# A new written-out order for all five engines, with two groups of constants of its planner changed

## The chip, the cores and the metric

The kernel runs as one program on one core of a Trainium2 chip. The metric is device time in microseconds (us). Before the change three runs took 282.60, 282.91 and 282.98 us, a median of 282.91. The interval that a repeat of this kernel stays in is about 0.2%, some 0.57 us.

## The reference

Eight batches of eight heads of decayed (retention) attention without softmax, 576 positions of 64 features each, feed a two-layer block with a gate `h * cos(h)`. The outputs of the attention are laid side by side by head, which gives 4608 tokens of 512 features.

```python
scores = scale * np.matmul(q, k.transpose(0, 1, 3, 2))
...
ret = scores * Dmat[None, :, :, :]
x = np.matmul(ret, v) ...        # 8 x 8 x 576 x 64, then 4608 x 512
h = x @ w_in                     # 512 x 2048
g = h * np.cos(h)
return (g @ w_out).astype(np.float32)   # 2048 x 512
```

## The kernel before

**Attention in units.** A unit is 256 positions of one batch with all its heads, named (batch, part); the last 64 positions of four batches make a unit of their own. For a unit q, k and v are loaded as float32 by SP (L585), turned into bf16 tiles `qnat`, `natk` and `natv` by POOL, DVE or ACT (L575, L624; v and q are multiplied by powers of the decay), and transposed, by TensorE in the first four units (L648) and by a DMA transpose in the others (L663). TensorE then makes scores (L694, `bk<-qt,kt`), DVE masks them (L743, `pt`), TensorE adds up the running states (L694, `bk<-natv,natk`, copied by ACT to `sba`, `sbb`, `sbr`) and the outputs (L694, `bk<-pt,natv` and `bk<-qt,sba`), and ACT and DVE copy these to `xt`. The matmuls of L694 are small, 64x64 weights with 64 or 128 columns, four of them side by side in the array, so that many instructions pass in a short time.

**Nine token blocks of 512.** Block j takes two units. The first layer is L908 (`bk<-xt,win`, with ACT's cosine in L917 and DVE's product in L920) in blocks 0 to 2, and a scheme of seven products instead of eight (L1037, with L1020, L1022 and L1026 for the gate) in blocks 3 to 8. The second layer uses seven products throughout: L1177 multiplies `gt`, sums `s` made by DVE (L1108, L1114) and weight sums `tw` (L1086); DVE and ACT put the result together in `os` (L1166, L574), and SP stores it (L1065). `win` and `wout` are each loaded in four slabs by POOL (L888, L892), as 512 KB of bf16 each, on the software DMA queue. Six loads of q, k and v go out at once; the loads of unit (0,1) wait until slab 2 of `win` has landed, since `unit((0, 1), gate=[("win", self.NEXT)])` has NEXT = 2, and the loads of unit (2,0) wait for slab 2 of `wout`.

**What sets the order.** `graph` makes some 1500 tasks, each for one engine. `lay` gives each task its rank from the table ORDER, two characters a task, and so fixes the order on each engine: an engine takes its tasks by rank, none overtakes another, and the semaphores follow from the data. `run` then goes through this order with planned times. These decide which buffer a task gets, how many idle matmuls (L517, `bk<-one`) are put in where TensorE is thought to wait, and which POOL operations are held back behind a DVE operation that ran shortly before (`push`). The table itself was found beforehand with the same planned times, and is written in as a constant.

**Instruction fetches in the planner.** TensorE's program is read in blocks of 256 instructions, where a matmul counts two (its weight load and itself) and a task some 0.2 to 0.4 for its waits. In `run` the fetch of block k is requested when instruction 128+256k is reached, and instruction 450+256k can't run before `usable[k]`. `FETCH` holds the times: 3200 ns after the request or 1500 ns after the planned end of the transfers, whichever is later, plus a last part.

**Slabs in the planner.** `load_w` gives each slab a time on the software queue (`dma`) and a time from its last packet to the semaphore (`tail`).

Of the kernel before, what the change touches and what calls it, by code (L numbers as in the profile page):

```python
# [371 lines left out]
class Kernel:  # L372
# [12 lines left out]
    ORDER = (
        "#####$#$#$#%#%#$#######%#&#&#%#$#&#'#)#(#'#)#,#+#'#.#7#/#*#/#'#+#*#,#(#-#.#&#&#%#*#)#(#-#(#)#*#0#2#0#1#3"
        "#2#1#,#7#V#8#/#7#'#(#,#)#-#.#G#@#K#H#*#0#/#L#C#J#G#+#2#1#+#N#O#K#L#M#N#P#E#S#P#T#H#Q#,#3#5#f#[#^#R#-#8#6"
        "#b#W#V#L#.#<#;#5#+#4#U#I#S#3#-#5#E#>#E#6#.#6#@#8#>#4#5#<#=#4#?#<#3#;#>#6#=#H#A#J#;#2#:#:#1#9#B#9#@#9#0#8"
        "#C#=#C#R#G#R#F#?#F#Q#F#P#I#B#I#D#<#D#A#:#A#?#;#B#M#D#O#4#7#9#:#/#>#=#0#?#@#1#A#G#6#m#o#j#k#m#l#l#_#r#u#s"
        "#a#`#_#d#y#p#^#i$'#w#]#Q#[#v#b#s$'#l$%$/#s$/#Z#N#W$3#v$1#e#Z#c$+#r$-#j#^#h$$#i#{#x#d#u$.#q$0#_#S#]$1#t$."  # L390
        "#[#O#X$(#m$&#W#J#T#{#h#|#\\#T#\\$*#n$)#Y#M#Y$&#k$(#|#g#x$,#p$+#X#K#U#y#f#z#a#U#`#z#j$##c#X#f#w#c#t#i#]#g$)"
        "#o$*#Z#b#V#a#q#e#o#n#`#d#Y#q#t#r#k#p#e#g#h#\\$#$%$$#n#u#v#8$-$0#w#O#2#D#B#5#I#C#3#E#H#<$5$7$7$9$8$3$6#z$?"
        "$$$#$@$%#|#4#9#F#K#7#J#N#=#;#M#L#C#:#>#O#R#A#Q#T#?#@#S#P#F$>$B$?$<$A$@$F$,$+$G$'$&$\\$?$Z$O$0$I$[$>$V$_$C"
        "$[$S$6$Q$U$7$P$K$*$D$Z$=$U$J$($G$M$-$J$L$1$L$R$5$N$Q$3$K$Y$<$T$X$:$R$T$@$Y$2$4$,$6$5$;$>$=$4$8#x$2$:$:$;"
        "$<#y$9$=#{$A$D$B$C$E$C#`$H$I$)#P$N$H$F$.$/$P$2$4$V$;$9$W$8$S#B#G#W#Z#E#X#V#D#M#Y#`#Q#J#N#^#a#H#c#[#I#L#\\"
        "#d#V$]$X$W$B$A$b$D$G$c$E$^$o$l$k$M$R${$Y$Z$|$W$s#S#K#f#l#R#e#j#U#X#g#o#[#T#\\#i#t#Y#w#x#W#Z#k#q#g%'$w$x$^"
        "$a%.$l$m%/$f$|#U$E#]$M#_$d#b$n$`$b$e$f$`$F$k$J$f$K$i$n$N$r$p$b#p$p$m$Q#h$y$V$t$s$O$t$P$x$U$r$v$S$z$u$[#n"
        "$w$q$X#m%($_$y%%$\\%&$]%*$e%#%)$`%-${$j#s%+$z$d#r%1$k%(%,$c%3$i%2$h%%%0$g%4%&$n#v%6%'$p#u%9$q%.$]$_$\\$a$c"
        "$o$O$g$d$e$H$^$a$h$h$i$I$g$j$L$l$m$j%#%$$v#o$q$u$T#f%)%+%1%/%=$r%>$s%@$v%5%A$t%D%8%%$(%B%4%,$*%L%$%?%E$y"
        "%G$|%M%#%>%H${%K%<%($&%N%=%.$)%P%&%A%S%*%U%-%Y%1%G%V%2%]%H%7$,%Z%F%<$.%d%=%P%[%3%_%6%`%9%L%^%5%c%K%>$1%e"  # L400
        "%N%E$2%g%?%Q%$%*%0%2%:%6%9%7%5%7$o%:%?%3%<%F$z%;%C$w%O%T%B%I%J%;$&%X%\\%4#q%8%-%,$u$x%Q%)%'%R%+%@#d#]#{#y"
        "#a$$#z#^#e$##|#i#b#k$%$0#h$3$-#_#c$'$+#v%W%D%C%/%0%a%8%:%b%;%J%M%S%V%T%k%B%m%D%o%G%[%n%C%q%Y%H$8%r%Z%K$<"
        "%u%M%b%z%N%{%O&'%S%e&$%P&(%d%W$?&%%c%Z$A&-%Y%i&&%R&)%U&*%T%f&,%V&3%j%`$C&.%h%c$D&6%e%q&/%X&1%]&2%\\%k&4%^"
        "&9%p%h$F&7%n%d$E&>%i%v%E%I%U%X%^%]%W%\\%f%i%A%p%x%`%l%t%L%j%s%I&#&+%g%y%|%a$?&0&5%_$=%h%O%R%@%F%v%Q%[%w%J"
        "%_#l#m$7$/#n$:$5#p#j$4$6#|#s#t$9$=#w$@$B#r#u$;$>$+&8%o%m%b%a&<%f%l&=%g%r%s%u%{%x&@%j&E%o&C%n%|&D%m&I&%%x"
        "$H&H&$%v$G&O%u&,&M%s&P%w&V&#&/&Q%y&W&1&($N&U&.&&$K&a&+&;&X&$&Y&%&[&'&6&]&*&c&5&1$P&\\&4&2$R&h&5&A&b&,&g&0"
        "&i&3&=&f&/&j&?&8$S&k&<&9$U&t&:&D%l%t%w&#&)%y&+&'&;&?%k&A&B%z&G&L%q&:&F%p&R&Z&0&K&N&*$7&^&`&-$:&J&&&(%r%t"
        "&S%z%{&T%|&-$-$6#z$4$I$L$%$,$8$0$J$O$##y#x#{$W$[$9&_&2&3&)&d&e&.&7&8&9&>&:&l&4&n&7&q&<&F&o&6&r&C&K$\\&s&B"
        "&@$Y&y&?&G&u&;&v&=&z&D&Q&x&A'&&K&L$_&{&H&C$X'*&I&R'#&B')&E'(&G&V''&F'/&W&O$`',&P&M$^'6&P&\\'4&N'5&Q'8&T&f"
        "'7&R';&]&X$a':&^&[$b'>&Z&h&@&E&I&L&M&J&S&N&m&p&>&|'$&O'%'-&J&w'+&H'0'2&Y'.'3&X$@'9'=&V$>$1$$$2$'$Q$V$)$5"  # L410
        "$*$($M$T$3$.$<$/$]$Z$;'1&[&T&Z&U'<&S&_&U&`&b&c&e&d'?&W'A&Y'B&\\&i'E&^'K&n&j$e'D&k&g$d'O&c&q'F&]'H&_'P&d&t"
        "'I&`'N&p&e$c'L&r&k$f'U&i&x'M&b'T&h'Q&o'#'W&l'[&w&p$g'Y''&y$i'^&r&{'Z&n'a&t'`&s'$']&q'b&|&u$h'f'+&z$j'e&v"
        "'&&a&l&j&m&g&v&s&o'@'G&a'S'V&u'R'X&m'C'J&f'\\'c'%'_'d'($A'i'j'#$C&y&z')','*'/'-'0'g'h&w&x'o'p'.$E$B'k'n&{"
        "&|'l'm'$'q'r'1'2$F$D's't'3'%'&'v'u'5'4$H$G"
    )
# [470 lines left out]
    def load_w(self, which, s, gate, prio):  # L886
        if which == "win":
            fn = lambda e: e.dma_start(  # L888
                ap(self.WIN, 4 * DFF, 0, 128, s * 512, [DFF, 4], [1, 512]),
                bass.AP(self.w_in, s * 512, [[DFF, 128], [128 * DFF, 4], [1, 512]]))  # L890
        else:
            fn = lambda e: e.dma_start(  # L892
                ap(self.WOUT, NF * DM, 0, 128, s * 4 * DM, [DM, 4], [1, DM]),
                bass.AP(self.w_out, s * 4 * 128 * DM, [[DM, 128], [128 * DM, 4], [1, DM]]))
# [456 lines left out]
```

## Time and profile before

| what | us |
|---|---|
| three runs, median | 282.91 (282.60 to 282.98) |
| the profiled execution, own time | 284.13 |
| its span, first to last instruction | 282.4 |
| what lies around the span | 1.73 |
| TensorE (PE) matmuls busy | 270.7 |
| PE waits for `win` by DMA | 0.9 |
| PE waits that the profile calls "issue", L694 and L908 | 2.4 and 0.7 |

The profile lists busy time by engine, groups of instructions by line, and the chain of work that ended last, followed back from the end: a share of a line in the chain is time in which nothing else could have ended the program earlier. "issue" is time in which an engine waited for nothing that the profile shows. A busy PE is not a PE at its peak, since matmuls are pipelined and their ends are modelled; the distance from one start to the next says more. In views of DMA, q1 is the queue of SP's transfers, q0 the software queue on which POOL's go, and q8 carries instructions. The granted clock of TensorE was 1.00 throughout.

### The profile page before, as it was taken

How to read it: one execution, taken by the hardware profiler on the slowest of the kernel's cores; microseconds unless marked ns; L12 is line 12 of the kernel's file. 1: busy time of each engine (PE TensorE's matmuls, PEld its weight loads, DVE VectorE, ACT ScalarE, POOL GpSimd, SP SyncE). 2: the span in 40 equal slices, each digit the busy share in tenths (PEclk: the TensorE clock that was granted, in tenths of full speed). 3: DMA queues.
4: the chain of work that ended last, by engine and by line, in shares of the span. 5: the costliest groups of instructions: out<-in, count | busy, mean ns of one | idle time of the engine just before them, and what ended most of it. 6: DMA issues, size and time to landing. Idle time of an engine off the chain costs nothing.

```text
span 282.4 us, 9745 instructions
## 1 busy us (share of the span) xinstructions
PE 270.7 (96%) x4136; PEld 219.9 (78%) x4136; DVE 227.3 (80%) x394; ACT 177.5 (63%) x367; POOL 161.2 (57%) x180
## 2 busy tenths in 40 slices
PE   6779989999999999979999999999999999999995
PEld 2457568888885468868888888888888888888884
DVE  3666889988974998868997996688759899997764
ACT  4346767255247765669469875885778865778530
POOL 4640872167377683897568757981375667216330
DMA  7999999999999999999999997979816090410016
GB/s 199 249 192 262 273 171 163 300 243 263 179 187 245 204 264 206 181 221 176 251 192 208 279 238 134 168 194 175 194 32 123 6 163 2 159 69 0 2 74 224
DMA packets 122731, 49.91 MB, mean 177 GB/s; under 512 B 84800, under 2 KB 118592, under 8 KB 122688
## 3 DMA queue, kind: packets, MB, share of 16 engines
q1 hardware_dynamic: 118176, 44.84, 74.8%
q0 software_dynamic: 4224, 4.19, 9.6%
q8 instruction: 32, 0.52, 0.8%
q10 hardware_dynamic: 288, 0.26, 0.3%
q14 instruction: 11, 0.09, 0.1%
HBM read 36.70 MB, written 9.44 MB: 163 GB/s over the span
## 4 chain that ended last, share of the span: by engine, by line
PE 84%; DMA 8%; POOL 3%; issue 2%; SPq 1%; DVE 1%; ACT 1%; DVEq 0%; ACTq 0%
PE bk L1177 38%; PE bk L1037 26%; PE bk L908 11%; PE bk L694 8%; DMA stgq<-in_q_dram 3%; DMA win<-in_moe_w_in_dram 3%; DMA stgk<-in_k_dram 3%; POOL natv L624 1%; SPq L585 1%; POOL qnat L624 1%; POOL gt L1026 1%; POOL win L888 0%; ACT xt L574 0%; DVE sq L1020 0%; PE bk L648 0%
## 5 line engine op out<-in xcount | busy, mean ns | idle before, releaser
L1026 POOL TENSOR_TENSOR gt<-sq,cb 128x512 bf16<-128x512 f32 x48 | 55.8, 1172 | 49.1 <-ACT cb L1022 27.0
L908 PE MATMUL bk<-xt,win 128*128 128x256 bf16 (+1 forms) x288 | 46.3, 308 | 1.8 <-DMA win<-in_moe_w_in_dram 0.9
L624 POOL TENSOR_TENSOR natv<-stgv,wv 128x512 bf16<-128x512 f32 x36 | 37.5, 1046 | 12.5 <-DVE s L1108 4.8
L920 DVE TENSOR_TENSOR gt<-bk,cb 128x256 bf16<-128x256 f32 (+1 forms) x72 | 34.5, 507 | 12.0 <-ACT cb L917 9.3
L917 ACT ACTIVATE cb<-bk 128x256 bf16<-128x256 f32 (+1 forms) x72 | 31.2, 455 | 19.6 <-PE bk L908 16.5
L624 POOL TENSOR_TENSOR qnat<-stgq,wq 128x512 bf16<-128x512 f32 x32 | 33.5, 1052 | 16.7 <-DVE s L1114 5.6
L1037 PE MATMUL bk<-xt,win 128*128 128x256 bf16 x288 | 41.0, 273 | 0.0
L1020 DVE TENSOR_TENSOR sq<-bk,sq 128x512 f32<-128x512 f32 x48 | 32.5, 684 | 8.9 <-PE bk L1037 5.0
L908 PEld LDWEIGHTS bk<-xt,win 128*128 128x128 bf16 x288 | 26.8, 98 | 15.3 <-DVE pt L743 1.2
L743 DVE TENSOR_TENSOR pt<-bk,tr 128x512 bf16<-128x512 f32 x48 | 31.1, 682 | 8.4 <-PE bk L694 8.1
L575 POOL CAST natk<-stgk 128x512 bf16<-128x512 f32 x34 | 20.7, 614 | 28.2 <-DMA stgk<-in_k_dram 15.7
L1177 PE MATMUL bk<-wout,gt 128*128 128x256 bf16 x288 | 36.7, 273 | 0.0
L1026 DVE TENSOR_TENSOR gt<-bk,cb 128x512 bf16<-128x512 f32 x48 | 32.3, 682 | 4.0 <-ACT cb L1022 3.8
L1177 PE MATMUL bk<-wout,s 128*128 128x256 bf16 x288 | 35.6, 273 | 0.0
L1177 PE MATMUL bk<-tw,s 128*128 128x256 bf16 x288 | 35.4, 273 | 0.0
L574 ACT ACTIVATE sq<-bk 128x512 f32<-128x512 f32 x48 | 27.7, 595 | 10.0 <-PE bk L1037 8.8
L1022 ACT ACTIVATE cb<-sq 128x512 bf16<-128x512 f32 x48 | 30.0, 632 | 5.4 <-DVE sq L1020 2.9
L1022 ACT ACTIVATE cb<-bk 128x512 bf16<-128x512 f32 x48 | 28.4, 598 | 6.7 <-PE bk L1037 3.7
L1177 PEld LDWEIGHTS bk<-tw,s 128*128 128x128 bf16 x288 | 28.0, 98 | 3.6 <-DVE pt L743 0.3
L1037 PEld LDWEIGHTS bk<-xt,win 128*128 128x128 bf16 x288 | 27.9, 98 | 3.6
L1177 PEld LDWEIGHTS bk<-wout,gt 128*128 128x128 bf16 x288 | 27.6, 98 | 3.7 <-issue 0.2
L1177 PEld LDWEIGHTS bk<-wout,s 128*128 128x128 bf16 x288 | 27.7, 98 | 3.5
(80 smaller groups left out, 436.5 us busy)
## 6 DMA issues: line engine op xcount, KB each, us to landing
stgq<-in_q_dram SPq DMA_DIRECT2D x16, 512.0 KB, 6.1
out_dram<-os SPq DMA_DIRECT2D x16, 512.0 KB, 4.4
stgk<-in_k_dram SPq DMA_DIRECT2D x20, 256.0 KB, 5.6
stgv<-in_v_dram SPq DMA_DIRECT2D x20, 256.0 KB, 5.4
stgk<-in_k_dram SPq DMA_DIRECT2D x6, 512.0 KB, 6.9
stgv<-in_v_dram SPq DMA_DIRECT2D x6, 512.0 KB, 7.4
win<-in_moe_w_in_dram POOLq DMA_DIRECT2D x4, 512.0 KB, 8.0
wout<-in_moe_w_out_dram POOLq DMA_DIRECT2D x4, 512.0 KB, 7.5
```

What stands on the lines that cost most here:

```text
L574: return self.one(eng, dur, lambda e: e.activation(dst(), src(), AF.Copy), r=r, w=w, **kw)
L624: self.one(eng, 610 if eng == "dve" else 1030, lambda e, out=out, inp=inp, tab=tab, col=col, hs=hs: e.tensor_tensor(out(), inp(), ap(tab, ...
L694: return lambda e: e.matmul(out(), lhs(), rhs(), start=start, stop=True, skip_group_check=True)
L743: self.one("dve", 610, lambda e, r=r, b=b, pt=pt: e.tensor_tensor(ap(self.at(pt), 1024, 0, 128, 512 * r, [64 * ny * ny, 8 // ny // ny], [1 ...
L908: inst = e.matmul(ap(self.at(bk), 512, 0, 128, 0, [1, n]), ap(self.WIN, 4 * DFF, 0, 128, c * DFF + 128 * f, [1, 128]), ap(self.at(xt), 204 ...
L917: self.one("act", n - 15, lambda e: e.activation(ap(self.at(cb), TB, 0, 128, 0, [1, n]), ap(self.at(bk), 512, 0, 128, 0, [1, n]), AF.Sin, ...
L920: self.one("dve", 75 + n / 0.96, lambda e: e.tensor_tensor(ap(self.at(gt), NF * TB, 0, 128, f * TB + 256 * h0, [1, n]), ap(self.at(bk), 51 ...
L1020: self.one("dve", 610, lambda e: e.tensor_tensor(half(src), self.at(bank).ap(), half(src), ALU.add), r=[(bank,)], w=four(src))
L1022: self.one("act", 530 if name else 490, lambda e: e.activation(self.at(cb).ap(), ap(self.at(src), size, 0, 128, 0, [1, 512]), AF.Sin, bias ...
L1026: self.one(eng, 1120 if name else 610, lambda e: e.tensor_tensor(ap(self.at(gt), NF * TB, 0, 128, (8 * n + 2 * g) * TB + 256 * h, [TB, 2], ...
L1037: inst = e.matmul(ap(self.at(bank), 512, 0, 128, 256 * f, [1, 256]), l(c, f), rr(c), stop=True, skip_group_check=True, start=(first and f ...
L1177: inst = e.matmul(place(bank, tt), l(f, tt), rr(f), stop=True, skip_group_check=True, start=(first and f == 0 and tt < len(bank)))
```

## The change

Three things change. The constants of the planned fetch get longer by 1500 ns, for requests before 45 us (4550 to 6050 ns) and after (2550 to 4050 ns). The planned slab times change from 2750 ns (`win`) and 3000 ns (`wout`) to 3350 ns for slab 0 of either and 2750 ns for the others, and slab 3 gets a tail of 2300 ns instead of 900. And ORDER is replaced as a whole. No task is added or taken away; beside the order, only the idle matmuls (24 before, 32 now) and the buffers that a task gets can differ. The table is cut to two lines here.

```diff
-    BACKLOG, FIRST = 4000, 6000
+    BACKLOG = 4000
     SHARES = (0.65, 0.30)
-    FETCH = (3200, 1500, 2550, 2000)
+    FETCH = (3200, 1500, 4050, 6050)
...
-                    usable[k] = max(a + self.FETCH[0], dma_free + self.FETCH[1]) + self.FETCH[2] + self.FETCH[3] * (a < 45000)
+                    usable[k] = max(a + self.FETCH[0], dma_free + self.FETCH[1]) + self.FETCH[2 + (a < 45000)]
...
     ORDER = (
-        "#####$#$#$#%#%#$#######%#&#&#%#$#&#'#)#(#'#)#,#+#'#.#7#/#*#/#'#+#*#,#(#-#.#&#&#%#*#)#(#-#(#)#*#0#2#0#1#3"
+        "#####$#$#$###%#$#####&#%#%#&#%#$#&#'#(#'#(#)#*#+#'#-#)#.#*#.#'#-#+#/#+#,#/#&#&#%#)#(#*#,#(#*#(#1#2#1#3#0"
...
-                 sem=f"{which}{s}", dma=2750 if which == "win" else 3000, tail=900, prio=prio)
+                 sem=f"{which}{s}", dma=3350 if s == 0 else 2750, tail=2300 if s == 3 else 900, prio=prio)
```

**TensorE between the outputs of unit (4,0) and the scores of unit (5,0)**, about 120 to 124 us of the profiled execution. `pt`, `natv`, `qt` and `sba` belong to the small matmuls of L694, `wout,s` to the second layer, and `xt` and `xs` to the first. In the kernel before stand the last small matmuls of the outputs, four rows of large matmuls, and the first of the scores:

```order
L694 MATMUL bk2<-qt2,sba2 64x64 x2
L1177 MATMUL bk7<-wout,s5 128x256 x8
L1177 MATMUL bk7<-wout,s6 128x256 x8
L1037 MATMUL bk2<-xt1,win 128x256 x4
L1037 MATMUL bk3<-xs0,tx1 128x256 x4
L694 MATMUL bk1<-qt0,kt1 64x64 x2
```

In the changed kernel the same place begins with:

```order
L694 MATMUL bk2<-qt2,sba2 64x64 x2
L1037 MATMUL bk1<-xt1,tx4 128x256 x4
L1037 MATMUL bk6<-xt1,win 128x256 x4
L1037 MATMUL bk0<-xs0,tx1 128x256 x4
L1177 MATMUL bk7<-wout,s3 128x256 x8
L1037 MATMUL bk6<-xs1,tx2 128x256 x4
L1037 MATMUL bk0<-xs2,win 128x256 x4
L1037 MATMUL bk1<-xt1,win 128x256 x4
L1037 MATMUL bk5<-xt1,win 128x256 x4
L1037 MATMUL bk6<-xt1,win 128x256 x4
```

Four more matmuls of L1037 follow before the scores, so that 44 large matmuls stand between the two runs of small ones where 24 stood.

**POOL at the start**, where it turns the first k and v into bf16 tiles and issues the four slabs of `win`. Before:

```order
L575 CAST natk1<-stgk1 128x512
L624 TENSOR_TENSOR natv0<-stgv0,wv 128x512
L888 DMA win<-in_moe_w_in_dram 128x4x512 x2
L624 TENSOR_TENSOR natv1<-stgv1,wv 128x512 x2
L888 DMA win<-in_moe_w_in_dram 128x4x512 x2
```

In the changed kernel:

```order
L575 CAST natk1<-stgk1 128x512
L624 TENSOR_TENSOR natv0<-stgv0,wv 128x512
L888 DMA win<-in_moe_w_in_dram 128x4x512
L624 TENSOR_TENSOR natv1<-stgv1,wv 128x512
L888 DMA win<-in_moe_w_in_dram 128x4x512
L624 TENSOR_TENSOR natv1<-stgv1,wv 128x512
L888 DMA win<-in_moe_w_in_dram 128x4x512 x2
```

The second slab now goes out behind one conversion of unit (1,0), the last two behind both. By the ranks in the two tables the slabs go out as 0, 2, 3, 1 before and as 0, 3, 2, 1 now.

More of the change, by code (lines that the diff above doesn't have):

```diff
@@ L391 @@
[L391 to L410, printed above, removed]
@@ new lines @@
+        "$e%5$k$l%6$m%)#R$F#]$H#`$d#a$p$^$b$j$f$]$B$f$G$b$F$h$k$L$q$n$P#g$o$l$U#i$x$W$t$s$Q$u$R$w$T$q$v$S$z$r$X#j"
+        "$y$s$^#n%$$[$v%%$\\%&$]%+$b%$%($`%,$z$d#r%)$y$j#s%1$i%(%*$a%2$h%/$g%%%-$c%0%&$q#u%4%'$p#t%9$r%.$_$a$]$`$c"
+        "$i$P$e$d$e$H$c$h$g$i$j$I$g$l$M$m$n$k${%'$x#h$r$t$V#d%*%,%2%0%8$o%?$v%;$s%4%>$u%B%7%##|%C%6%-$,%I%(%?%E$y"
+        "%F$z%H${%:%J$|%M%<%)$%%K%;%%$(%P%+%A%S%,%T%.%X%2%F%W%0%\\%H%:$.%Y%E%9$/%a%;%P%[%3%b%8%`%7%K%_%6%d%M%A$0%g"
+        "%O%E$2%i%@%S$w${%1%3%9%+%8%=%3%7$n%=%A%5%<%G%$%@%D$w%Q%U%B%L%R%@$/%Z%e%<#p%:%/%-$t$x%N%*%&%O%'%>#c#`#{$)"
@@ new lines @@
+        "#b$*#z#^#a#v$&#m#f#e$#$'#j$+$3#_#i$$$1#v%V%C%D%/%1%]%4%=%^%5%I%J%L%R%Q%h%?%n%F%m%G%Y%k%B%o%W%O$7%q%X%H$5"
+        "%s%L%_%x%N%|%R&%%S%e%{%Q&$%b%Z$?&&%c%X$@&+%W%g&'%T&)%U&*%V%f&,%Y&0%j%\\$C&.%i%`$D&5%d%q&/%[&7%a&2%]%m&4%_"
+        "&8%o%i$F&:%p%e$E&;%h%t%G%N%V%Z%`%\\%d%]%c%f%>%v%w%^%j%z%P%p%r%J&(&-%h%y&#%a$*&1&6%c$@%l%T%U%C%D%t%K%M%u%I"
+        "%[#q#l$6$8#n$9$4#r#k$:$-$+#t#o$;$>#w$<$=#u#s$B$A$.&3%k%l%^%b&<%g%m&=%f%s%u%x&%&#&?%k&D%r&C%l%y&F%n&J&'%y"
+        "$I&L&*%|$K&N%u&+&M%t&U%z&Q%w&-&P%v&V&/&&$N&X&1&*$P&h&2&?&Y&%&Z&$&`&,&5&^&(&c&7&4$R&_&4&-$Q&l&8&A&a&+&b&."
@@ L415 @@
+        "'K&a'P&s&g$e'L&o&c$c'T&j&v'N&f'S&h'X&r'%'U&i'Y&w&s$g'W&z&z$j']&q&{'Z&m'[&o'_&t'$'^&p'a&|&v$h'b')&w$i'd&u"
+        "''&X&i&j&m&a&q&x&p'?'A&`'Q'R&u'V'\\&n'E'J&k'`'f'&'c'i'*$A'l'o'$$D&y'+'(','#'/'-'0'h'j&x&y'e'p'.$B$C'm'n&|"
+        "&{'g'k'#'q'r'2'1$E$F's'u'4'%'&'v't'5'3$H$G"
     )
```

23 lines of the change are left out of this document (15 added, 8 removed).

## The prediction

> **What bounds the kernel now.** I read the page's busy times and chain first, to see which engine ends the work.
>
> ```profile
> PE 270.7 (96%) x4136; PEld 219.9 (78%) x4136; DVE 227.3 (80%) x394; ACT 177.5 (63%) x367; POOL 161.2 (57%) x180
> q8 instruction: 32, 0.52, 0.8%
> PE 84%; DMA 8%; POOL 3%; issue 2%; SPq 1%; DVE 1%; ACT 1%; DVEq 0%; ACTq 0%
> ```
>
> TensorE is the chain, but for the start. No matmul of the computation is added or taken away, so all that an order can change is time in which TensorE stands still. Its waits, longest first, show what that is:
>
> ```profile
> PE bk L694 <- issue: 2.4, 3, 1.5
> ...
> PE bk L908 <- DMA win<-in_moe_w_in_dram: 0.9, 1, 0.9
> PE bk L908 <- issue: 0.7, 1, 0.7
> ```
>
> The largest, 2.4 + 0.7 = 3.1 us, is a wait for nothing that the trace names. The timeline of TensorE gives the places:
>
> ```profile
> 20.40 0.50 PE L908 MATMUL bk<-xt,win 128*128 128x256 bf16 x3 [0.68 <-issue]
> ...
> 38.22 0.22 PE L694 MATMUL bk<-natv,natk 64*64 64x64 bf16 x3 [0.71 <-issue]
> ...
> 125.45 0.25 PE L694 MATMUL bk<-natv,natk 64*64 64x64 bf16 x7 [1.46 <-issue]
> ```
>
> The second and third fall in the midst of one group of small matmuls, where no data is awaited. The DMA view, asked in stretches of 0.1 us, shows what ends them. These are its q8 lines from 18.0, 35.7, 44.3, 114.0 and 122.6 us on:
>
> ```profile
> q8 instruction: 1, 0.02, 58.4%
> q8 instruction: 1, 0.02, 64.3%
> q8 instruction: 1, 0.02, 63.4%
> q8 instruction: 1, 0.02, 79.9%
> q8 instruction: 1, 0.02, 71.7%
> ```
>
> Each is one packet of some 16 KB, and there are 32 (0.52 MB) for TensorE's 2 x 4136 instructions: blocks of 256. Packets at 18.0, 35.7 and 122.6 stand 2.4, 2.5 and 2.85 us ahead of the three restarts. So the stalls are late instruction blocks. Numbering the blocks from 0, these are blocks 0, 2 and 13.
>
> When was each asked for? The code counts the request at instruction 128+256k. By the order, that is reached near these rows (timeline twice, then the chain) for blocks 2, 3 and 13, at 29.8, 37.1 and 117.4 us:
>
> ```profile
> 29.98 0.39 PE L648 MATMUL bk<-idn,natk 128*128 128x128 bf16 x4
> ...
> 36.63 0.64 PE L694 MATMUL bk<-pt,natv 64*64 64x128 bf16 x32
> ...
> 117.73 2.18 PE bk L1037 x20
> ```
>
> From request to use: block 2 38.22 - 29.8 = 8.4 us; block 3 44.3 + 2.6 - 37.1 = 9.8; block 13 125.45 - 117.4 = 8.05. Block 14, whose packet came at 127.3 on a request at 123.9, had 3.4 + 2.7 = 6.1. The middle of a fetch is thus the wait for its packet, 3 to 7 us, which differs from place to place.
>
> **The change, part by part.** *Block 13.* From request to need are 322 instructions, 161 matmuls. A large one costs 0.109 us, from the chain's last run:
>
> ```profile
> 265.58 13.99 PE bk L1177 x128
> ```
>
> By counting rows, before had 46 large and 115 small ones there; the stall began 6.6 us after the request, so a small one takes (6.6 - 46 x 0.109) / 115 = 0.014 us. The changed order has 81 large and 80 small: 8.8 + 1.1 = 9.9 us, more than the 8.05 that the fetch took. **Term: -1.46** (0 if that fetch is slower by 3.3 us).
>
> *Block 14.* It now has 54 large and 107 small: 5.9 + 1.5 = 7.4 us. With block 13's 8.05 it stalls 0.65, with its own 6.1 not at all. *Block 3* has 67 large and 94 small: 7.3 + 1.3 = 8.6 us; with its own 9.8 it stalls 1.2, with block 13's 8.05 not at all. I take about half of each: **+0.3 and +0.4** (0 to 1.9 together).
>
> The Trainium skill's page Runtime: NRT & Kernel Launch, section Instruction fetch mechanics, has the same blocks of 16 KiB with 256 instructions, but holds that crossing into the next is "mostly hidden". The stall of 1.46 us at 125.45 differs from it in this case; by that rule alone the sum would lack the terms of blocks 13, 14 and 3.
>
> *Switches.* Going from small to large matmuls costs 0.98 - 0.87 = 0.11 us, by the chain:
>
> ```profile
> 101.16 0.98 PE bk L1177 x8
> ...
> 103.44 0.87 PE bk L1177 x8
> ```
>
> The order has 72 changes between kinds instead of 76. I price each way alike: **-0.4** (0 to -0.5).
>
> *The start.* The rows of POOL, SP and TensorE, and the landing of the third slab's issue (from the DMA view at 14 to 16):
>
> ```profile
> 12.00 1.71 POOL L888 DMA_DIRECT2D win<-in_moe_w_in_dram  x2
> 13.94 2.04 POOL L624 TENSOR_TENSOR natv<-stgv,wv 128x512 bf16<-128x512 f32 x2 [0.23 <-DMA stgv<-in_v_dram]
> 15.93 1.55 POOL L888 DMA_DIRECT2D win<-in_moe_w_in_dram  x2
> ...
> win<-in_moe_w_in_dram POOLq DMA_DIRECT2D x1, 512.0 KB, 7.8
> ...
> 21.24 0.37 SPq L585 DMA_DIRECT2D stgk<-in_k_dram  x1
> ...
> 21.88 8.26 PE L908 MATMUL bk<-xt,win 128*128 128x256 bf16 x56
> ...
> 32.23 2.04 POOL L624 TENSOR_TENSOR natv<-stgv,wv 128x512 bf16<-128x512 f32 x2
> ...
> 33.58 0.64 PE L694 MATMUL bk<-qt,kt 64*64 64x128 bf16 x32
> ...
> 38.58 0.61 PE L908 MATMUL bk<-xt,win 128*128 128x256 bf16 x4
> ```
>
> Slab 2, second before, landed by 21.24, where SP starts the loads of unit (0,1). Now it is third; the third landed at 15.93 + 7.8 = 23.7. The issues move from 12.86 to 14.95 and from 15.93 to 16.8, but the queue was never empty between, so I keep 23.7. Three things follow.
> - *SP's six loads* are issued 2.5 us later. But what did the early issue buy? The DMA view of 23.0 to 24.0 us has q0 alone, q1 appears at 24.6, and after SP's issue at 47.55 it appeared within 1 us:
>
> ```profile
> q0 software_dynamic: 203, 0.21, 123.8%
> ...
> q1 hardware_dynamic: 63, 0.03, 57.2%
> ...
> 47.55 0.37 SPq L585 DMA_DIRECT2D stgk<-in_k_dram  x1
> ...
> q1 hardware_dynamic: 3, 0.00, 2.3%
> ```
>
> So the loads waited for the slabs anyway, and 23.75 + 1.0 = 24.75 against 24.5 makes 0.25 us. POOL's last `natv` of the unit ends near 34.6 instead of 34.3.
> - *TensorE's second group* of the other half needs slab 2 and waits for 23.7. Ahead of the scores are then 40 matmuls of 256 columns, 24 of 512 and 16 transposes: 4.4 + 24 x 0.218 + 16 x 0.055 = 10.5 us (by columns from the 0.109), hence scores at 34.2. Before, 44, 24 and 16 such took from 21.88 to 33.58, 11.7 us for 10.9 of work; with that loss of 0.8 again it is 35.0.
> - From the scores to the end of the outputs, where L908 goes on, it took 38.58 - 33.58 = 5.0 us with the stall of block 2 (0.71). Block 2 now has 19 large matmuls of 256 columns, 35 of 512 and 107 small: 2.1 + 7.6 + 1.5 = 11.2 us against 8.4, so no stall; one idle matmul adds 0.2. That gives 4.5, and the outputs end at 38.7 to 39.5. **Term: +0.4** (-0.3 to +0.9).
>
> The stall of block 0 (0.68) goes too, since the request comes 2 us earlier; TensorE then waits for `xt` and slab 2 instead, so it gains nothing: 0.
>
> The Trainium skill's page DMA: Bandwidth & Descriptors, section Queues, rings and completion order, has each DMA engine go round robin between its queues, packet by packet. The lines above, q1 empty with loads issued, differ. By that rule the loads would have moved from about 22.2 on, and the 2.5 us would be lost.
>
> *`wout`.* Slabs 2 and 3 go out behind two and three more conversions, some 1.5 and 2.5 us later:
>
> ```profile
> 38.96 1.55 POOL L892 DMA_DIRECT2D wout<-in_moe_w_out_dram  x2
> ...
> wout<-in_moe_w_out_dram POOLq DMA_DIRECT2D x2, 512.0 KB, 9.5
> ```
>
> They took 9.5 us, most of it behind slabs 0 and 1, which cover the delay: 0, and up to +2.5 if the queue runs dry.
>
> *The end.*
>
> ```profile
> 277.84 0.69 DVE L1166 TENSOR_TENSOR os<-bk,sn 128x512 f32<-128x512 f32 x1 [0.94 <-PE bk L1177]
> 278.56 1.31 ACTq L1065 DMA_DIRECT2D out_dram<-os  x2
> 278.71 0.42 DVE L575 COPY os<-bk 128x256 f32<-128x256 f32 x1 [0.18 <-PE bk L1177]
> ```
>
> The sum that ACT stores now closes eight matmuls (0.87 us) later, between the two copies, and its two stores go out to about 280.7 instead of 279.87: **+0.2** (0 to +0.8).
>
> **Sum:** -1.46 + 0.3 + 0.4 - 0.4 + 0.4 + 0.2 = -0.56. The profiled execution, 284.13 (282.4 and 1.73 around), becomes 283.57; the median, 1.2 us below it, 282.91 becomes **282.3**.
>
> **The rivals.**
> 1. *The stalls come back at other blocks, and it is slower.* Blocks 4, 7, 15 and 17 have 60, 56, 66 and 64 large matmuls, which gives 8.0, 7.6, 8.5 and 8.3 us. Block 12's packet came at 114.0 on a request at 108.2, in the row
>
> ```profile
> 107.52 3.49 PE bk L1177 x32
> ```
>
> which makes 5.8 us, and with 2.85 a fetch of 8.65. At that pace these four, with block 14's 1.25 and block 3's 1.2, lose 0.65 + 1.05 + 0.15 + 0.35 + 2.45 = 4.65, 3.95 more than the sum holds; half of that gives 284.3. For it: the waits follow the transfers queued ahead, which the order moves too. Against it: in the kernel before one block of 28 stalled after 45 us. It decides from stalls of 1.9 us in all.
> 2. *The late slab 2 costs its 2.5 us in full*, if the loads' 3.3 us from issue to first packet are their own and not q0's. Then POOL ends `natv` at 36.8 and the outputs end 2.2 us late instead of 0.4: 284.1. The lines of q0 and q1 speak against it. The DMA page's rule leads here too.
> 3. *Nothing new stalls and the start costs nothing*: -1.46 - 0.4 + 0.2, 281.2.
> 4. *The fetches don't follow the planned times at all*: the 1.46 stays in some form and no other comes, +0.4 - 0.4 + 0.2: 283.1. Against it stands the packet 2.85 us ahead of the restart. The Runtime page's rule leads here as well.
>
> **How the numbers follow.** My forecast has 0.40, with a range of its own from 281.6 to 283.1; rival 1 0.24, rival 2 0.09, rival 3 0.19, rival 4 0.08. A measurement tells 0.2%, 0.57 us, from no change: the limits are 282.34 and 283.48. The forecast lies on the lower one and gives 0.22 faster, 0.15 same, 0.03 slower; rival 1 0.04 same and 0.20 slower, rival 2 0.09 slower, rival 3 0.19 faster, rival 4 0.01 faster, 0.04 same and 0.03 slower. Faster 0.42, same 0.23, slower 0.35. The range runs from 280.9, rival 3 with a better start, to 284.4, rivals 1 and 2.
>
> **What would show it.** Right: no "issue" wait near the scores of unit (5,0); q8 packets of blocks 13 and 14 over 2.9 us ahead of their need; SP's seventh load at about 23.7 and q1 right behind it; scores of unit (0,1) at 34.2 to 35.0. Wrong: "issue" waits over 1.5 us in all, q1 starting only at 27, or TensorE waiting on DVE, ACT or POOL after 45 us, which this sum holds at zero.

## The result, and the profile after the change

The changed kernel took 284.35 us in the median (283.77 to 285.18, 7 runs), the kernel before 282.91 (282.45 to 283.73, 7 runs). The ratio is 1.0054, with a 95% interval from 1.0036 to 1.0072: slower by 0.5%, where 282.3 was forecast. A second measurement, a_again below, gave 1.0036 (1.0014 to 1.0057). The profiled execution took 285.18, the longest of the seven, with a span of 283.5 (before: 284.13 and 282.4). Three runs below each had one execution in a slow state (1545 us in a_again, 551 in a_gate, 394 in a_early_again), which their ratios leave out.

The page of the changed kernel: busy times, and the shares of the chain.

```profile
PE 272.8 (96%) x4144; PEld 219.8 (78%) x4144; DVE 231.2 (82%) x394; ACT 177.3 (63%) x367; POOL 162.9 (57%) x180
PE 78%; DMA 8%; DVE 6%; POOL 4%; SPq 2%; issue 1%; ACT 1%; DVEq 0%
```

TensorE's share of the chain fell from 84% to 78%, DVE's rose from 1% to 6%, POOL's from 3% to 4%. TensorE's waits show the same exchange (us in total, times, longest):

```profile
PE bk L908 <- DMA win<-in_moe_w_in_dram: 1.8, 1, 1.8
...
PE bk L1177 <- DVE s L1114: 0.5, 1, 0.5
```

"issue", 3.1 us before, is not among them any more. At the scores of unit (5,0) the small matmuls now run in one piece, in TensorE's timeline:

```profile
129.49 0.45 PE L694 MATMUL bk<-qt,kt 64*64 64x64 bf16 x32
129.76 0.30 PE L694 MATMUL bk<-natv,natk 64*64 64x64 bf16 x16
```

In its place stand a wait for `win` twice as long and a wait for DVE. The first, in the timelines of POOL, SP and TensorE:

```profile
11.98 0.96 POOL L888 DMA_DIRECT2D win<-in_moe_w_in_dram  x1
14.00 1.03 POOL L624 TENSOR_TENSOR natv<-stgv,wv 128x512 bf16<-128x512 f32 x1 [1.06 <-DMA stgv<-in_v_dram]
14.99 0.81 POOL L888 DMA_DIRECT2D win<-in_moe_w_in_dram  x1
15.82 1.05 POOL L624 TENSOR_TENSOR natv<-stgv,wv 128x512 bf16<-128x512 f32 x1
16.81 1.55 POOL L888 DMA_DIRECT2D win<-in_moe_w_in_dram  x2
...
25.16 0.37 SPq L585 DMA_DIRECT2D stgk<-in_k_dram  x1
...
25.19 5.48 PE L908 MATMUL bk<-xt,win 128*128 128x256 bf16 x44 [1.82 <-DMA win<-in_moe_w_in_dram]
...
35.81 0.42 PE L694 MATMUL bk<-qt,kt 64*64 64x128 bf16 x16
...
38.86 0.64 PE L694 MATMUL bk<-pt,natv 64*64 64x128 bf16 x32
```

Slab 2 landed at 25.15, not at 23.7; SP and TensorE follow at once. The outputs of unit (0,1) start at 38.86 instead of 36.63 (37.1 in b_wout and b_nohold below, whose start is that of the kernel before). The software queue q0 moved this in 20.0 to 21.5 us, after and then before (packets, MB, busy share):

```profile
q0 software_dynamic: 177, 0.18, 91.0%
```

```profile
q0 software_dynamic: 307, 0.31, 124.7%
```

The second wait, with POOL's issues of `wout`, SP's first load of unit (2,0) and its conversion on POOL:

```profile
36.51 1.55 POOL L892 DMA_DIRECT2D wout<-in_moe_w_out_dram  x2
...
41.62 0.80 POOL L892 DMA_DIRECT2D wout<-in_moe_w_out_dram  x1
...
44.27 0.80 POOL L892 DMA_DIRECT2D wout<-in_moe_w_out_dram  x1
...
49.32 0.37 SPq L585 DMA_DIRECT2D stgk<-in_k_dram  x1
...
55.22 1.69 POOL L575 CAST natk<-stgk 128x512 bf16<-128x512 f32 x2 [10.15 <-DMA stgk<-in_k_dram]
55.34 2.11 DVE L1114 TENSOR_TENSOR s<-gt 128x1024 bf16<-128x1024 bf16 x2
57.38 1.53 DVE L1086 TENSOR_TENSOR tw<-wout,tw 128x1024 bf16<-128x1024 bf16 x1
59.43 1.15 DVE L1114 TENSOR_TENSOR s<-gt,s 128x1024 bf16<-128x1024 bf16 x1
60.64 1.92 PE L1177 MATMUL bk<-wout,s 128*128 128x256 bf16 x16 [0.46 <-DVE s L1114]
```

In the kernel before, POOL's `natk` was done ahead of these sums, and they took 0.68 us each:

```profile
51.99 1.17 POOL L575 CAST natk<-stgk 128x512 bf16<-128x512 f32 x2 [7.02 <-DVE pt L743]
...
54.36 0.68 DVE L1114 TENSOR_TENSOR s<-gt 128x1024 bf16<-128x1024 bf16 x1
```

Now they take up to 1.53 while POOL converts what SP loaded late; and there the chain runs over DVE (by line, 55 to 62 us):

```profile
by line: DVE s L1114 44.5%; DVE tw L1086 20.8%; PE bk L1177 19.6%; DVE os L1166 8.6%; DVE wout L1086 8.6%; issue 0.7%
```

### The profile page after: what moved, and what is told of

Same layout as the page of the kernel before. It is cut to its first block, busy times and chain, and to the rows that moved or that the text cites. A ratio compares the mean times of both kernels' runs of the same rounds, so it can differ in the third digit from the quotient of the medians.

```text
span 283.5 us, 9767 instructions
## 1 busy us (share of the span) xinstructions
PE 272.8 (96%) x4144; PEld 219.8 (78%) x4144; DVE 231.2 (82%) x394; ACT 177.3 (63%) x367; POOL 162.9 (57%) x180
## 4 chain that ended last, share of the span: by engine, by line
PE 78%; DMA 8%; DVE 6%; POOL 4%; SPq 2%; issue 1%; ACT 1%; DVEq 0%
PE bk L1177 37%; PE bk L1037 26%; PE bk L908 8%; PE bk L694 7%; DMA win<-in_moe_w_in_dram 3%; DMA stgv<-in_v_dram 3%; DMA stgq<-in_q_dram 2%; SPq L585 2%; POOL qnat L624 1%; DVE tw L1086 1%; DVE s L1114 1%; POOL natv L624 1%; DVE gt L920 1%; DVE pt L743 1%; DVE s L1108 1%
## 5 line engine op out<-in xcount | busy, mean ns | idle before, releaser
L1026 POOL TENSOR_TENSOR gt<-sq,cb 128x512 bf16<-128x512 f32 x48 | 55.2, 1156 | 39.7 <-ACT cb L1022 19.4
L624 POOL TENSOR_TENSOR qnat<-stgq,wq 128x512 bf16<-128x512 f32 x32 | 34.2, 1075 | 18.2 <-DMA stgq<-in_q_dram 13.7
L1037 PE MATMUL bk<-xt,win 128*128 128x256 bf16 x288 | 41.3, 273 | 0.0
L575 POOL CAST natk<-stgk 128x512 bf16<-128x512 f32 x34 | 21.4, 638 | 34.3 <-DMA stgk<-in_k_dram 28.7
L917 ACT ACTIVATE cb<-bk 128x256 bf16<-128x256 f32 (+1 forms) x72 | 30.6, 457 | 15.7 <-PE bk L908 13.2
L743 DVE TENSOR_TENSOR pt<-bk,tr 128x512 bf16<-128x512 f32 x48 | 30.9, 681 | 10.5 <-PE bk L694 10.4
L908 PEld LDWEIGHTS bk<-xt,win 128*128 128x128 bf16 x288 | 26.4, 98 | 16.9 <-DMA win<-in_moe_w_in_dram 2.1
L920 DVE TENSOR_TENSOR gt<-bk,cb 128x256 bf16<-128x256 f32 (+1 forms) x72 | 33.8, 505 | 6.9 <-ACT cb L917 3.3
L1177 PE MATMUL bk<-wout,s 128*128 128x256 bf16 x288 | 36.4, 273 | 0.5 <-DVE s L1114 0.5
L1177 PE MATMUL bk<-tw,s 128*128 128x256 bf16 x288 | 36.0, 273 | 0.0
L1037 PEld LDWEIGHTS bk<-xt,win 128*128 128x128 bf16 x288 | 27.7, 98 | 3.7
```

Of the source, the lines that this page charges most:

```text
L575: return self.one(eng, dur, lambda e: e.tensor_copy(dst(), src()), r=r, w=w, port=eng == "pool", **kw)
L624: self.one(eng, 610 if eng == "dve" else 1030, lambda e, out=out, inp=inp, tab=tab, col=col, hs=hs: e.tensor_tensor(out(), inp(), ap(tab, ...
L743: self.one("dve", 610, lambda e, r=r, b=b, pt=pt: e.tensor_tensor(ap(self.at(pt), 1024, 0, 128, 512 * r, [64 * ny * ny, 8 // ny // ny], [1 ...
L908: inst = e.matmul(ap(self.at(bk), 512, 0, 128, 0, [1, n]), ap(self.WIN, 4 * DFF, 0, 128, c * DFF + 128 * f, [1, 128]), ap(self.at(xt), 204 ...
L917: self.one("act", n - 15, lambda e: e.activation(ap(self.at(cb), TB, 0, 128, 0, [1, n]), ap(self.at(bk), 512, 0, 128, 0, [1, n]), AF.Sin, ...
L920: self.one("dve", 75 + n / 0.96, lambda e: e.tensor_tensor(ap(self.at(gt), NF * TB, 0, 128, f * TB + 256 * h0, [1, n]), ap(self.at(bk), 51 ...
```

## The experiments

**Theory.** The stall of block 13 went as forecast. What costs is POOL's order of slab issues: at the start slab 2 lands late, and in `wout`'s stage the software queue runs slow, the loads of unit (2,0) and POOL's conversions come late, and these fall on DVE's sums, for which TensorE waits. **Rivals:** the loss lies elsewhere (end, switches, constants); only one of the two places counts; conversions are slow by themselves, not by coming late.

Labels with a_ change the changed kernel, those with b_ the kernel before. Edits of ranks go in right behind `self.G.lay(self.ORDER)`, where `task(key)` finds the task that writes a key and `rank(engine)` gives an engine's tasks by rank; those of a_gate and b_nohold go in behind `order = self.G.run()`. Ratios are to the kernel before on the same chip, with 95% intervals (0.001 is 0.28 us). A ratio is known to some 0.002, so a difference between two of them only to some 0.003, or 0.8 us.

| run | what | ratio |
|---|---|---|
| a_again | changed kernel | 1.0036 (1.0014 to 1.0057) |
| a_swap | slabs 2 and 3 of `win` exchanged | 1.0037 (1.0013 to 1.0061) |
| a_win | slab 2 right behind slab 0 | 1.0004 (0.9986 to 1.0022) |
| a_wout | slabs 2, 3 of `wout` earlier | 0.9987 (0.9966 to 1.0008) |
| a_both | a_swap and a_wout | 0.9993 (0.9974 to 1.0012) |
| a_early | a_win and a_wout | 0.9958 (0.9940 to 0.9976) |
| a_early_again | the same | 0.9966 (0.9948 to 0.9984) |
| a_gate | loads of (2,0) wait for slab 1 | 1.0005 (0.9985 to 1.0024) |
| a_wout_tail | a_wout, old end | 1.0020 (0.9999 to 1.0042) |
| a_early_tail | a_early, old end | 0.9985 (0.9962 to 1.0008) |
| b_swap | slabs 2 and 3 of `win` exchanged | 1.0074 (1.0047 to 1.0101) |
| b_wout | slabs 2, 3 of `wout` later | 0.9996 (0.9971 to 1.0021) |
| b_shift | blocks shifted | 1.0009 (0.9982 to 1.0036) |
| b_const | new constants alone | 1.0093 (1.0063 to 1.0123) |
| b_nohold | two holds taken away | 1.0001 (0.9976 to 1.0026) |

TensorE's order is the same in all a_ kernels up to the end, so the start of one group can be compared. From the timelines, the start of the outputs (`bk<-pt,natv`) of three units, and the end of TensorE's last group:

| profile | (0,1) | (1,1) | (2,0) | last |
|---|---|---|---|---|
| changed kernel | 38.86 | 55.15 | 77.48 | 280.21 |
| a_again | 38.07 | 53.89 | 76.23 | 279.22 |
| a_win | 37.26 | 53.13 | 75.65 | 278.41 |
| a_wout | 38.03 | 54.24 | 75.46 | 277.87 |
| a_early | 37.16 | 53.37 | 74.54 | 277.10 |

From (2,0) to the last all take 202.4 to 203.0 us: what differs is made before 78 us. The first column follows slab 2 of `win`; from (1,1) to (2,0) it is 22.3, 22.3 and 22.5 us with `wout` as in the change, 21.2 with it early. (In a_swap, whose profiled execution was 1.3 us above its median, it is 23.7.)

**The changed kernel again.** 

> The changed kernel once more, unaltered, so that the others of this call stand beside it on one chip, and a second profile of it, since the starts of two kernels with the same order differed by 0.8 us in their profiles. Theory (wout's stage costs it about 1.5 us, the start some tenths that vary with the landing of slab 2): 0.5% above the kernel before, DVE's sums between 54 and 61 us again stretched by POOL. Rival (the first profile was an accident): no stretched sums in it.

The stretched sums are there again (L1086 1.53 us, TensorE waits 0.41 for it), the start is 0.8 us better: slab 2 let SP go at 24.38 and TensorE at 24.41. So about 0.8 of the first profile's start was that execution's own. In three more profiles with slab 2 third in the new order, SP went at 24.33 (a_wout), 24.20 (a_gate) and 23.73 (a_wout_tail).

**Slab 2 second, by exchange with slab 3.**

```diff
+        a, b = task("win", 2), task("win", 3)
+        a.prio, b.prio = b.prio, a.prio
```

> The changed kernel with slabs 2 and 3 of win exchanged, so that slab 2 goes out second as before; nothing else differs. Theory (the start is what costs: slab 2 landed at 25.15 instead of 21.2, and all behind it is 1.4 us later): slab 2 lands at about 20.5, TensorE's second group starts at 23.4 instead of 25.19, scores of unit (0,1) at 34.2 instead of 35.8, and the time is 1.4 us less, 283.0. Rival 1 (the loads of unit (0,1), not slab 2, hold the start, and they queue behind all four slabs anyway): TensorE waits later instead, under 0.4 us less, 284.0. Rival 2 (the loss is in wout's stage and at the end): no change, 284.3.

Nothing gained, although slab 2 landed at 20.49. In TensorE's timeline the wait has moved on to the last slab:

```profile
28.71 1.90 PE L908 MATMUL bk<-xt,win 128*128 128x512 bf16 x12 [1.78 <-DMA win<-in_moe_w_in_dram]
```

So the rank of slab 2 isn't all of it: the last slab was late too. In 20 to 21.5 us q0 moved 200 packets here, against 303 in a_win below, where the first two slabs go out together. Why the queue slows is not shown.

> The kernel before with slabs 2 and 3 of win exchanged, so that slab 2 goes out third as in the changed kernel (four idle matmuls are put in where TensorE now waits). Theory (a late slab 2 costs the start what it delays TensorE's second group): slab 2 lands at about 23.7, the group starts at 23.8 instead of 21.88, and the time is 1.3 to 1.9 us more, 284.2 to 284.8. The prediction's own step (the start loses 0.4 only, since the loads of unit (0,1) wait for the slabs anyway): 283.3. Rival (no loss at all, TensorE's other waits take it up): 282.9.

In the kernel before the same exchange costs 2.1 us (1.3 to 2.9, six executions). There two slabs go out at once, and slab 2, third, let SP go at 23.86, near the 23.7 that the prediction had for a third slab; TensorE's second group starts at 23.98 instead of 21.88, and the outputs of (0,1) at 38.55 instead of 36.63. The prediction's step, by which a slab 2 that lands at 23.7 costs 0.4, fails here: the outputs of (0,1) lose what TensorE's second group loses. Not all of the 2.1 need be the slab's, though, since the planner moves 21 of POOL's holds with it; in the profile the outputs of (1,1) start only 1.1 us later (55.38 against 54.28).

**Slab 2 right behind slab 0.**

```diff
+        task("win", 2).prio = task("win", 0).prio + 0.3
```

> The changed kernel with slab 2 of win right behind slab 0, and wout as in the change. Theory (the start's loss and that of wout's stage add up): TensorE doesn't wait for slab 2, outputs of unit (0,1) at 37.2 instead of 38 to 38.9, 0.8 us less than the changed kernel; DVE's sums near 55 to 60 are stretched as in the changed kernel: 1.001 to 1.003 of the kernel before. Rival (what the start gains is lost again in wout's stage, since POOL's conversions and DVE's sums meet the harder): as the changed kernel, 1.004 to 1.005.

The queue stays full (303 packets in 20.0 to 21.5 us), SP goes at 20.05, and the outputs of (0,1) start at 37.26. 0.0032 to 0.0050 of the time go, 0.9 to 1.4 us, and the sums stay stretched (L1086 1.53 us, TensorE waits 0.5), so the start's loss and that of `wout`'s stage stand apart. Idle matmuls, holds and buffers are those of the changed kernel: only the slab's place differs.

**`wout` early.**

```diff
+        pool = rank("pool")
+        at = pool[pool.index(task("wout", 1)) + 2].prio
+        for s in (2, 3):
+            task("wout", s).prio = at + 0.3 * (s - 1)
```

> The changed kernel with slabs 2 and 3 of wout issued right behind the two qnat conversions, ahead of one natk and two natv; nothing else differs. Theory (the software queue ran dry, the loads of unit (2,0) came 1.8 to 2.4 us late, POOL's conversions of them fell on DVE's sums of bf16, and DVE ran 2.1 us late into TensorE's wait at 60.6): the last slab lands some 2 us earlier, SP's loads of unit (2,0) go out at about 47.5, DVE's L1114 and L1086 between 55 and 60 take their usual 0.68 us each, TensorE's wait for s at 60.6 goes, 0.8 us less: 283.5. Rival 1 (POOL and DVE meet by the order, whenever the loads come): the long DVE rows stay, no change, 284.3. Rival 2 (natv behind the slabs is late for TensorE): 0.5 us more.

0.0049 to 0.0067 go, 1.4 to 1.9 us, more than expected (0.0050 against a_swap, on the same chip). The timelines:

```profile
39.07 1.55 POOL L892 DMA_DIRECT2D wout<-in_moe_w_out_dram  x2
...
47.01 0.37 SPq L585 DMA_DIRECT2D stgk<-in_k_dram  x1
...
52.18 1.17 POOL L575 CAST natk<-stgk 128x512 bf16<-128x512 f32 x2 [6.86 <-DVE tw L1086]
...
53.83 1.08 DVE L1086 TENSOR_TENSOR wout<-wout 128x1024 bf16<-128x1024 bf16 x1
54.83 1.28 DVE L1114 TENSOR_TENSOR s<-gt 128x1024 bf16<-128x1024 bf16 x2
56.03 0.68 DVE L1086 TENSOR_TENSOR tw<-wout,tw 128x1024 bf16<-128x1024 bf16 x1
57.87 0.68 DVE L1114 TENSOR_TENSOR s<-gt,s 128x1024 bf16<-128x1024 bf16 x1
58.81 1.91 PE L1177 MATMUL bk<-wout,s 128*128 128x256 bf16 x16
```

POOL's `natk` is done before DVE's sums, all but one of these (1.08) take about 0.68 us, and TensorE doesn't wait. What q0 moved in 43 to 47 us, with slab 2 issued at 40.63 and slab 3 at 43.02 (a_again), and with both at 39.07 (a_wout):

```profile
q0 software_dynamic: 549, 0.54, 101.3%
```

```profile
q0 software_dynamic: 829, 0.82, 124.2%
```

The planner follows the new ranks here: eight of POOL's holds and the buffers of 74 tasks differ from the changed kernel too. What they do to the time was not tried by itself.

> The changed kernel with both exchanges: slab 2 of win second, and slabs 2 and 3 of wout ahead of natk and natv. Theory: the two losses are apart from each other, and 1.4 + 0.8 = 2.2 us go, 282.2. Rival 1 (both are one chain: with the start earlier, POOL and DVE no longer meet, so that the second exchange has nothing left to gain): as the first exchange alone. Rival 2 (neither is the cause): 284.3.

As a_wout alone: the exchange brings nothing here either, for the reason of a_swap.

**`wout` late in the kernel before.**

```diff
+        pool = rank("pool")
+        n = pool.index(task("wout", 1))
+        for s in (2, 3):
+            task("wout", s).prio = pool[n + 2 + s].prio + 0.5
```

> The kernel before with slabs 2 and 3 of wout issued behind one natv and the other, as in the changed kernel; nothing else differs. Theory (the software queue runs dry behind slabs 0 and 1, the loads of unit (2,0) come 2 to 3 us late, POOL's conversions of them are late and fall on DVE's sums): SP's loads of (2,0) at about 50 instead of 47.55, 1 to 2 us more, 283.9 to 284.9. The prediction's own step (slabs 0 and 1 cover the delay): 282.9. Rival (the order of DVE in the kernel before leaves room, so that late loads are made up for): 283.2 at most.

Nothing is lost, but the last rival's case, late loads that are made up for, didn't arise, since the loads went out on time. Slabs 2 and 3 were issued one by one, within 0.2 us of their times in a_again, and yet q0 moved far more in 43 to 47 us than the 549 packets there:

```profile
40.47 0.80 POOL L892 DMA_DIRECT2D wout<-in_moe_w_out_dram  x1
...
42.96 0.80 POOL L892 DMA_DIRECT2D wout<-in_moe_w_out_dram  x1
```

```profile
q0 software_dynamic: 742, 0.74, 119.0%
```

SP's first load goes out as in the kernel before (47.56). `natk` comes 1.4 us later (53.35), the two sums beside it are stretched to 1.00 and 1.09 only, and TensorE doesn't wait for them. So issuing these two slabs singly doesn't by itself slow q0, and what slows it in the changed kernel stays open. In that kernel slabs 0 and 1 go out together (35.34 in a_again), here singly (35.27 and 37.65); whether that is the reason was not tried.

**Loads of (2,0) a slab earlier.**

```diff
+        for t in order:
+            for p in t.parts if t.eng == "sp" else ():
+                p[2][:] = [("wout", 1, 0) if x == ("wout", 2, 0) else x for x in p[2]]
```

> The changed kernel, in which SP's loads of unit (2,0) wait for slab 1 of wout instead of slab 2; the order and the buffers stay as they are. SP issues them some 4 us earlier, at 44 to 45, while the software queue still holds two slabs. Theory (POOL's conversions come late because the loads do, and fall on DVE's sums): if the loads' packets move beside the slabs', natk is converted by 52, DVE's sums keep 0.68 us and 0.8 to 1.1 us go: 283.4 where the changed kernel has 284.4. Rival 1 (the loads' queue stays empty as long as the software queue has packets, as at 22 to 24.5 us of the kernel before): packets only at about 49.5, nothing gained, 284.4. Rival 2 (both queues share, and what the loads gain the slabs lose): tw is late on DVE instead, 284.4 or more.

Half of it: SP issues at 43.51, `natk` is converted at 53.17 instead of 54.09 (a_again), one sum is still 1.54 us, and (1,1) to (2,0) takes 21.7 us. TensorE's wait of 0.4 is a new one, and rival 2 holds in part: `tw` is late on DVE, since its slab is.

```profile
52.04 0.69 DVE L1086 TENSOR_TENSOR tw<-wout,tw 128x1024 bf16<-128x1024 bf16 x1 [0.70 <-DMA wout<-in_moe_w_out_dram]
...
52.79 1.05 PE L1177 MATMUL bk<-tw,s 128*128 128x256 bf16 x8 [0.43 <-DVE tw L1086]
```

The DMA view shows why the early issue brings the loads so little, at 46 to 47 and 48 to 49 us:

```profile
q0 software_dynamic: 100, 0.10, 88.6%
...
q0 software_dynamic: 140, 0.14, 87.7%
q1 hardware_dynamic: 116, 0.06, 29.2%
```

For over 3 us after the issue q1 moves nothing, though q0 doesn't use the engines fully; then both move side by side.

**POOL and DVE at once, with nothing late.** In the kernel before, two waits on DVE (`push`) are dropped:

```diff
+        stg = [self.staged[x, (2, 0)] for x in "kqv"]
+        for t in order:
+            if any(x[0] in stg for p in t.parts for x in p[2]):
+                t.parts[0][4].pop("push", None)
```

> The kernel before without two waits that the planner puts in (push): POOL's first natk and first qnat of unit (2,0) no longer wait for a DVE operation that ran shortly before, and so start when their loads have landed, natk some tenths and qnat some 2 us earlier. Nothing is later than before. Theory (what costs TensorE there is that POOL's conversions and DVE's sums of bf16 run at the same time and stretch each other, not that the conversions are late): qnat starts at about 54 instead of 56.33, L1114 and L1086 between 53.8 and 57 take up to 1.5 us instead of 0.68, TensorE waits for DVE near 58, 0.9 to 1.5 us more than the kernel before. Rival (lateness is what costs): earlier conversions cost nothing, no difference or some tenths less.

The rows come out as the theory says:

```profile
52.96 2.50 POOL L624 TENSOR_TENSOR qnat<-stgq,wq 128x512 bf16<-128x512 f32 x2 [0.61 <-DMA stgq<-in_q_dram]
53.40 1.15 DVE L1114 TENSOR_TENSOR s<-gt,s 128x1024 bf16<-128x1024 bf16 x1
54.47 1.53 DVE L1114 TENSOR_TENSOR s<-gt 128x1024 bf16<-128x1024 bf16 x1
55.93 1.53 DVE L1086 TENSOR_TENSOR wout<-wout 128x1024 bf16<-128x1024 bf16 x1
...
58.72 2.36 PE L908 MATMUL bk<-xt,win 128*128 128x256 bf16 x20 [0.94 <-DVE os L1166]
```

Conversions that come earlier stretch the sums just the same, so what stretches them is that both run at once; TensorE waits 0.94. In the profile the outputs go from (1,1) to (2,0) in 24.0 us against 23.2 before, so 0.8 is lost there. But the time is that of the kernel before, as the rival had it. In this profile the 0.8 is made up elsewhere (a stall of block 13 of 1.1 instead of 1.46 is part of it); whether that is usual isn't settled.

The Trainium skill's page SBUF — State Buffer, section Who interferes with whom, has a rule for it: a DVE instruction with two inputs in SBUF and a GpSimd instruction that reads SBUF exclude each other, whoever is first runs to its end. The traces agree: 1.53 instead of 0.68 for DVE where POOL was first, and 2.90 instead of 1.17 for POOL's two casts in a_again, where DVE was.

**Shifted blocks.** 28 idle matmuls of 4 columns are added:

```diff
-            for _ in range(n):
-                inst = e.matmul(self.at(self.wb).ap(), self.ONE.ap(), ap(self.ONE, 128, 0, 128, 0, [0, 4], [1, 128]),
+            for c in [128] * n + [1] * (28 if n > 10 else 0):
+                inst = e.matmul(ap(self.at(self.wb), 512, 0, 128, 0, [c, 4], [1, c]), self.ONE.ap(), ap(self.ONE, 128, 0, 128, 0, [0, 4], [1, c]),
```

> The kernel before with 28 short idle matmuls of 4 columns more, some 0.06 us each, at the end of the first run of idle matmuls, where TensorE waits for data anyway: the blocks of 256 instructions shift by 28 matmuls, nothing else. Theory (the stalls are late instruction blocks, and how late depends on the work between request and need): by the order block 13 gets 7.8 instead of 6.0 us of work there and block 2 13 instead of 9.6, so the stalls of 1.46 near 125 and 0.71 near 38 go; block 0 has 4.3 instead of 5.0 and stalls up to 0.7 more; blocks 14 and 17 have 6.1 and 6.5 and may stall up to 0.6 each. In all 0.9 to 1.5 less, 281.7. Rival (the stall near 125 is a wait of another kind, tied to its place in the work): it stays where it is, 282.9.

The stall at block 13 is gone, by the shift alone:

```profile
123.44 0.45 PE L694 MATMUL bk<-qt,kt 64*64 64x64 bf16 x32
123.69 0.32 PE L694 MATMUL bk<-natv,natk 64*64 64x64 bf16 x16
```

and block 2's too: the stalls are late blocks. The time isn't less, though 0.9 to 1.5 us less was expected, so that a stall's removal buys its length in time is not shown. In this profile the last large store took 4.6 us instead of 3.1 and added 1 us at the end, and TensorE waited 0.9 for `wout`; whether that is usual with the shift stays open. In the three profiles of the old order with unshifted blocks the stall of block 13 was 1.46, 0.64 (b_wout) and 1.1 (b_nohold), 1.1 in the mean. With four idle matmuls more (b_swap) it was 0.80, with seven (b_const, next) 1.8.

**The constants alone.**

```diff
-    FETCH = (3200, 1500, 2550, 2000)
+    FETCH = (3200, 1500, 4050, 2000)
...
-                 sem=f"{which}{s}", dma=2750 if which == "win" else 3000, tail=900, prio=prio)
+                 sem=f"{which}{s}", dma=3350 if s == 0 else 2750, tail=2300 if s == 3 else 900, prio=prio)
```

> The kernel before with the new constants alone (fetch and slab times) and its own table: 7 idle matmuls more at the start and a few moved, all where the planner expects TensorE to wait, and the blocks of instructions shift by 14. Theory (the constants do nothing but through the table that was found with them): 282.7 to 283.3, no difference from the kernel before on the same chip. Rival (idle matmuls delay what TensorE has next): 0.5 to 1.5 us more.

2.6 us more, in four executions; the rival holds and doesn't suffice. Idle matmuls cost the start 0.3 to 0.9 (outputs of (0,1) at 37.43, against 36.52 to 37.14 in four profiles with the old constants). But the planned times also move the holds: POOL now converts beside three sums of DVE, 1.5 us each, and TensorE waits 1.3 for `os`. So the constants act without the table.

**The end.**

```diff
+        for e in ("pe", "dve"):
+            a, b = rank(e)[-3:-1]
+            a.prio, b.prio = b.prio, a.prio
```

> The changed kernel with slabs 2 and 3 of wout ahead of natk and natv, and with the last halves on TensorE and DVE in the order of before (the two halves of P3 and then the two of P4, the sum ahead of both copies). Theory (the end costs 0.45): 0.45 less than with wout alone, 282.6 where the kernel before has 283.4 on the chip of the last call. Rival (the two stores of ACT end beside the others either way): the same as with wout alone.

> The changed kernel with slab 2 of win right behind slab 0 and slabs 2 and 3 of wout ahead of natk and natv, once more, as the control of the next. Theory (the gain of 0.4% over the kernel before is real): 0.9940 to 0.9976 of the kernel before. Rival (it was that chip): 0.998 or more.

> The same with the last halves on TensorE and DVE in the order of before. Theory (the changed end costs 0.45 us: 3.3 us from TensorE's last matmul to the end of the span instead of 2.85): 0.3 to 0.5 us less than its control. Rival (the sum's two stores end no later than the store of the last copy either way): within 0.2 us of its control.

With a_early and the old end (a_early_tail) the profile has 2.9 us from TensorE's last group to the span's end, against 3.2 to 3.3 in all profiles with the new end, but the time is no less than that of its control, 0.9985 against 0.9966. With a_wout and the old end the last store took 5.0 us, and the ratio is 1.0020 against 0.9987. The expected gain isn't there.

**A version that beats both.**

> The changed kernel with slabs 2 and 3 of wout ahead of natk and natv, and with slab 2 of win issued right behind slab 0, so that both conversions of unit (1,0) come 0.8 us later. Theory (with wout's stage mended, the late slab 2 still costs the start some tenths): slab 2 lands by 21.5, TensorE doesn't wait for it, and the time is 0.4 to 0.9 us under that of the run with wout alone: 282.2 to 282.7 where the kernel before has 283.4. Rival 1 (the whole queue sets the start, since slab 1 is needed third whatever comes second): as with wout alone, 283.1. Rival 2 (natv is later by the issue of a slab, and TensorE waits for that): up to 0.8 us more.

0.9958 and, on another chip, 0.9966: 1.0 to 1.2 us below the kernel before, 2.0 to 2.7 below the changed one. TensorE doesn't wait for slab 2, and of DVE's sums there only one, of 1.07 us, is stretched. Only the ranks of three slab issues were changed, with what the planner makes of them, so the changed kernel's loss lies in POOL's order.

## Why the prediction was wrong, by its steps

- **Block 13, -1.46.** The stall is gone in every profile of the new order. Its size was one execution's; three give 1.1. That the time gains this isn't shown by itself: b_shift took the stall away and gained nothing.
- **Blocks 14 and 3, +0.7.** They didn't stall: 0. Rival 1, which had stalls come back, is refuted (the most in any profile of the new order is 0.5, at block 2 in a_wout_tail), and with it rival 4.
- **Switches, -0.4.** Not measured by themselves.
- **The start, +0.4.** Mis-sized, by two assumptions. "The queue was never empty between, so I keep 23.7" was too early: q0 ran slow at 20 to 21.5 us, and in five profiles SP went at 25.16, 24.38, 24.33, 24.20 and only once at 23.73. And the gains set against it (block 2's stall, 0.8 of idle time) didn't pay for the wait: a_win has 0.9 to 1.4 us for it, a_early against a_wout 0.6 to 0.8. The 10.5 us from slab 2 to the scores were right (10.6), so was q1 behind the slabs. Rival 2 named slab 2 with 2.5 us, too much.
- **`wout`, 0.** This is the step that failed. "Most of it behind slabs 0 and 1, which cover the delay": they didn't. SP's loads, released by slab 2, went at 49.32 and 48.38 in the two profiles of the changed kernel, at 47.01 with the slabs early. It costs 1.4 to 1.9 us (a_wout), 1.1 to 1.3 with the start mended (a_early against a_win). The prediction had the bound, "+2.5 if the queue runs dry", but followed the slabs only to their landing, not to the loads behind them, POOL's conversions of these, and DVE, and no rival held it. "TensorE waiting on DVE, ACT or POOL after 45 us" was named as what would show it wrong, and it is what came. Why q0 ran slow is open: in b_wout it didn't, with slabs 2 and 3 issued at the same times.
- **The end, +0.2.** 0.45 by the profiles, none in the time.

With the measured sizes, -1.1 - 0.4 (as forecast) + 0.6 to 1.4 + 1.1 to 1.9 + 0 to 0.45 gives +0.2 to +2.3, where 1.0 to 1.5 were measured: it fits, but too widely to prove the terms that no run measured. With both losses of POOL's order mended, a_early stands at -1.0 to -1.2, halfway between the forecast's -0.56 and rival 3's -1.66.

How much of `wout`'s loss is DVE's stretch and how much the late conversions themselves isn't settled: a_gate takes off half of both, and b_nohold shows a stretch that the time doesn't.

## What to carry to other kernels

Follow a delayed transfer past its landing: to what its landing releases, to the engine that handles that, and to the operations that will now run at the same time; a delay that is covered at the queue can come back two engines later. Look at a queue's pace stretch by stretch, and not only at the order of its transfers: a queue that isn't empty can still move at two thirds of its pace. And size a stall by several executions before its removal is counted in full.
